# A fused attention, MoE and FFN kernel: stores moved to another queue, small loads moved later, a table's product moved one step

## The chip, the cores and the metric

The kernel runs on one core of a Trainium2 chip. A core has five engines that run their own instruction streams: PE (TensorE, matmuls and transposes), ACT (ScalarE), DVE (VectorE), POOL (GpSimd) and SP (SyncE, which here only starts transfers). The metric is device time in microseconds (us) of one execution.

## The reference, cut to what matters

```python
# attention: q, k, v are [4, 8, 576, 64]; heads 0-3 local, 4-7 strided
mask_local = (rel >= 0) & (rel < 32)
mask_strided = (rel >= 0) & (pos[None, :] % 32 == pos[:, None] % 32)
scores = where(mask, q @ k.T / 8, -1e9);  attn = softmax(scores) @ v
x = attn.transpose(0, 2, 1, 3).reshape(2304, 512)
# MoE: 8 experts, top 1, F = 1024
logits = x @ w_gate + modality_bias[modality_id]
e_idx = argmax(logits);  gate_w = softmax(logits)[e_idx]
out[mask_e] = gate_w[mask_e] * (relu(x[mask_e] @ w1[e]) @ w2[e])
# dense FFN, 512 -> 2048 -> 512
h = out @ w_in;  g = where(h > 0, h, exp(min(h, 0)) - 1);  result = g @ w_out
```

## The kernel before

The program has three stages: attention (to about 131 us of the trace), the mixture of experts (to about 383 us) and the dense FFN (to the end). Every instruction's order on its engine is the order in which the code is written; an engine runs its stream in order and waits where a semaphore says so.

**Attention** runs over 32 steps n, two for each of 16 pairs of heads (four batches; in each, two strided pairs and then two local ones). Step n emits, in this order: S(n), the scores, into two PSUM banks of the tag "S", which has two, so that S(n) has to wait until DVE has copied step n-1's scores out of them (`sm`, L1027) with the mask added; T, the transposes of the next pair's `qn` and `kn` (L996, bank `ps_tr`, one half before and one after PT), which ACT copies to `qt` and `kt`; PT(n-2), the transposes of the exponentials; L, the router's logits; X(n-5), transposes of finished rows of x, which ACT casts to `xh` and DVE to `xl`; PV(n-3), the product with v, which DVE scales into `xs`; and the exponential of step n-1 on ACT. POOL subtracts the row maxima (L1035). The loads of a pair (`load_pair`, L890 and L895) are started on SP some five steps ahead. When a batch's rows of a pair of heads are ready in `xs`, `emit_PV` stores them to `x_dram` in HBM, on SP (L1103 strided, L1106 local; 12 stores).

**The router's early work** stands in a background generator. `bg()` emits its next piece, `bg.step()` starts a new step, and a yielded STEP ends what may be emitted in this step. It starts in step 21: `choose` (logits to expert), `early` (which expert and where each token goes, then a table of the first job's rows, made by `onehot` and `oa` on DVE, `A` on POOL and nine small matmuls `tab_ps` on PE, L404, whose result DVE turns into `idx` and `gates`), then four indirect gathers on POOL (`xg`, L459), the casts of the first weights (`split_to`), four scalings by the gate on DVE (L463) and four groups of transposes on PE (`trans`, L474, bank `x_ps` of the tag "T", which has two). The table's product is the call `finish()`. In the kernel before, steps 25 to 31 hold: 25 `finish` and gathers 0 and 1; 26 gathers 2 and 3 and `split_to(0)`; 27 `split_to(1)`; 28 scalings 0 and 1; 29 scalings 2 and 3 and `trans` 0; 30 `trans` 1 and 2; 31 `trans` 3.

**The router's small inputs** are `wgf` (the gate's weights, 16 KB), `mi` (modality ids, 18 KB) and `bb` (the two bias rows). They are loaded on ACT's queue as its first instructions; `wgs` (first used by L in step 10) and `mf` come from them at once, and `emit_bias` in step 5 makes the bias of each token, with three operations and the constants of the router on POOL.

**The MoE** runs as a stream of numbered pieces, and the list `plan` puts other work (the last attention steps, the other tables, gathers, transposes) before the piece of a given number.

Transfers started from SP and ACT signal their landing on eight semaphores in turn, DMAHW0 to DMAHW7. An instruction that starts a transfer waits until the last one on its semaphore has landed.

Of the kernel before, what the change touches and what calls it, by code (L numbers as in the profile page):

```python
# [73 lines left out]
class Background:  # L74
# [99 lines left out]
class Router:  # L174
# [105 lines left out]
    def early(self, pool, chosen, more):  # L280

        V = self.tc.nc.vector
        t = lambda shape, dt, name: pool.tile(shape, dt, name=name)
        rank = self.rank(NE, 1)
        yield
        key = t([128, E], F32, "key")
        kmax = t([128, 1], F32, "kmax")
        z = t([128, NE, E], F32, "z")
        pr = t([128, NE, E], F32, "pr")
        no = t([128, NE], F32, "no")  # L290
        sh = [128, NE, E]
# [12 lines left out]
        yield Background.STEP
        V.reduce_sum(pos, pr, axis=AX.X)
        V.tensor_tensor(key[0:1], key[0:1], self.rev[0:1], ALU.mult)
        yield
        V.tensor_scalar(pos, pos, 4096.0, None, ALU.add)
        V.reduce_max(kmax[0:1], key[0:1], axis=AX.X)
        yield  # L310
        V.tensor_scalar(self.star, kmax[0:1], -1.0, float(E), ALU.mult, ALU.add)
        chosen()
        yield from self.split_places(0, NE)
        yield Background.STEP
        onehot = self.new_onehot(pool)
        for i, _ in enumerate(self.onehot(0, NE, onehot)):
            yield
        finish = self.table(pool, onehot, 0, NE, 0, 4, 5, self.idx, self.gates, self.tc.nc.gpsimd)
        more()
        yield Background.STEP  # L320
        finish()
        yield

        def others():

            V.tensor_scalar(no, pos, 512.0, None, ALU.is_ge)
            V.tensor_scalar(self.oh[:, 0:NE, 0], pos, 512.0, None, ALU.is_lt)
            V.tensor_tensor(oh, oh, no.unsqueeze(2).to_broadcast(sh), ALU.mult)

        self.others = others  # L330
# [84 lines left out]
def ffn(tc, ctx, x_dram, part_dram, ident, router, conv, bank, w1, w2, out, run_attention):  # L415
# [187 lines left out]
    def early():  # L603
        STEP = Background.STEP
        yield from router.choose(0, NE)
        yield STEP
        yield from router.early(r_p, lambda: fetch_to(0), lambda: fetch_to(1))
        for c in range(4):
            gather(jobs[0], c)
            yield STEP if c == 1 else None  # L610
        split_to(0)
        fetch_to(2)
        yield STEP
        split_to(1)
        fetch_to(3)
        yield STEP
        for c in range(4):
            scale(jobs[0], c)
            yield STEP if c == 1 else None
        for kk in range(4):  # L620
            trans(jobs[0], kk)
            yield STEP if kk % 2 == 0 else None

    bg.early = early
    at = run_attention(bg)
# [17 lines left out]
    def more_tables(c0):  # L643
        fin.append(router.table(late[0], oh[0], 0, NT, c0, c0 + 16, 5, idx, gate))
# [21 lines left out]
    def stream():  # L666
# [31 lines left out]


    plan = [  # L700
        (2, lambda: at.PV(29)), (1, lambda: at.X(27)), (2, lambda: at.X(28)), (2, lambda: at.PT(30)),
        (3, lambda: at.PV(30)), (3, lambda: at.X(29)), (3, lambda: at.PT(31)),
        (4, lambda: at.PV(31)), (4, lambda: at.X(30)),
# [1 line left out]
        (10, lambda: at.lg(NE, NT)), (5, lambda: router.others()), (10, lambda: run(router.choose(NE, NT))), (10, close_b),  # L705
        (14, lambda: run(router.place(r_p))), (16, first_tables),
        (28, table), (28, lambda: router.blocks(r_p)), (28, lambda: new_job(1)), (66, open_y),
        (84, lambda: more_tables(20)), (100, table), (104, lambda: more_tables(36)), (116, table), (164, table),
    ]
    plan += [(120 + 4 * i, lambda i=i: dense(i)) for i in range(NT // 3 + 1)]  # L710
    plan += [(28, lambda c=c: gather(jobs[1], c)) for c in range(4)]
    plan += [(38, lambda c=c: scale(jobs[1], c)) for c in range(4)]
    plan += [(n, lambda kk=kk: trans(jobs[1], kk)) for kk, n in enumerate((47, 50, 53, 55))]
# [144 lines left out]
def attention(tc, bg, q, k, v, mod, mbias, wg, x_dram, ident, router, bank):  # L858
# [105 lines left out]
    m0 = const.tile([128, NT], F32, name="m0")  # L964
    bias = const.tile([128, NT, E], F32, name="bias")
    bt = const.tile([128, NT, E], F32, name="bt")
    nc.scalar.dma_start(wgf, wg.rearrange("(k p) e -> p k e", p=128))
    nc.scalar.dma_start(mi, mod.bitcast(I32).rearrange("(i p two) -> i p two", p=128, two=2))
    nc.scalar.dma_start(bb, mbias.rearrange("m e -> (m e)").partition_broadcast(128).rearrange("p (m e) -> p m e", m=2))

    nc.scalar.copy(wgs[:, :, 0:E], wgf)
    nc.vector.tensor_tensor(wgs[:, :, E:2 * E], wgf, wgs[:, :, 0:E].bitcast(F32), ALU.subtract)
    nc.vector.tensor_copy(mf, mi[:, :, 0])

    def emit_bias():
        pm = bank("T", "pm", 128, NT)
# [7 lines left out]
        router.constants()  # L984

    st = {}

    def emit_T(pi, j):

# [58 lines left out]
            nc.scalar.copy(pt[0:w, nj * r:nj * r + nj], ps)  # L1048
        st[n] = pt

    xs = {}

    xh, xl = (xt_p.tile([128, 4, S], F32R, name=nm) for nm in ("xh", "xl"))
    lgt = const.tile([2 * E, 2 * S], F32, name="lgt")
# [1 line left out]
    def emit_PV(n):  # L1056
        b, pr, s = steps[n]
        m, w, nj = shape(pr)
        pt = st.pop(n)
        key = (b, pr // 2)  # L1060
        if key not in xs:
            xs[key] = xs_p.tile([m, S // m, 4 * D], F32, tag=f"xs{pr // 2}", name="xs")
        c0 = 2 * (pr % 2) * D
        xv = xs[key][:, nj * s:nj * s + nj, c0:c0 + 2 * D]
        rs = m_p.tile([m, 2, nj], F32, tag="rs", name="rs")
        if pr >= 2:
            pss = [bank("P", "ps_v", m, nj, D + 1) for r in range(2)]
        else:

            both = bank("P", "ps_v", m, 2 * nj, D + 1)  # L1070
            pss = [both[:, nj * r:nj * r + nj] for r in range(2)]
        for r in range(2):
            for j in range(nj):
                if pr >= 2:
                    vv = vs[:, 2 * (pr % 2) + j % 2, 4 * s + 2 * (j // 2) + r]
                else:
                    vv = vl[:, nj * s + j, 2 * (pr % 2) + r]
                nc.tensor.matmul(pss[r][:, j], lhsT=pt[:, nj * r + j], rhs=vv, start=True, stop=True)
            if pr >= 2:
                nc.vector.tensor_scalar(rs[:, r], pss[r][:, :, D], 1e-9, None, ALU.add)  # L1080
                bg()
        if pr < 2:
            nc.vector.tensor_scalar(rs.rearrange("p r j -> p (r j)"), both[:, :, D], 1e-9, None, ALU.add)
            bg()
        bg()
        nc.vector.reciprocal(rs, rs)
        bg()
        if pr >= 2:
            for r in range(2):
                o = xv.rearrange("p (g r) (h d) -> p g r h d", r=2, h=2)[:, :, r]  # L1090
                nc.vector.tensor_tensor(o, pss[r][:, :, 0:D].rearrange("p (g h) d -> p g h d", g=2),
                                        rs[:, r].rearrange("p (g h) -> p g h", g=2).unsqueeze(3).to_broadcast([m, 2, 2, D]), ALU.mult)
                bg()
        else:
            nc.vector.tensor_tensor(xv.rearrange("p j (r d) -> p r j d", r=2), both[:, :, 0:D].rearrange("p (r j) d -> p r j d", r=2),
                                    rs.unsqueeze(3).to_broadcast([m, 2, nj, D]), ALU.mult)
            bg()
            bg()
        if pr % 2:
            xb = x_dram[b * S:(b + 1) * S]  # L1100
            if pr >= 2:
                if s == 1:
                    nc.sync.dma_start(xb[:, 4 * D:].rearrange("(m a) c -> m a c", a=G), xs[key])  # L1103
            else:
                g = slice(nj * s, nj * s + nj)
                nc.sync.dma_start(xb[:, 0:4 * D].rearrange("(i p) c -> p i c", p=m)[:, g], xs[key][:, g])  # L1106

    def emit_X(n):

        b, pr, s = steps[n]  # L1110
        m, w, nj = shape(pr)
        c0 = 2 * (pr % 2) * D
        ps = bank("P", "ps_x", 128, nj, m)
        for g in range(nj):
            nc.tensor.transpose(ps[:, g], xs[b, pr // 2][:, nj * s + g, c0:c0 + 2 * D], ident[0:m, 0:m])

        def view(t):
            t = t[:, pr]
            if pr >= 2:
                return t.rearrange("p (m a) -> p a m", a=G)[:, 4 * s:4 * s + 4]  # L1120
            return t.rearrange("p (i m) -> p i m", m=m)[:, nj * s:nj * s + nj]

        nc.scalar.copy(view(xh), ps)
        nc.vector.tensor_tensor(view(xl), ps, view(xh).bitcast(F32), ALU.subtract)
        bg()
        bg()
# [16 lines left out]

    for j in range(4):
        emit_T(0, j)
    NU = len(steps)
    LP, LV, LX = 2, 3, 5
    for n in range(NU):
        emit_S(n)
        if n + 2 < NU:  # L1150
# [16 lines left out]
        bg.step()  # L1167
        if n:
            emit_exp(n - 1)
        if n == 5:  # L1170
            emit_bias()
        if n % 2 == 1:
            p = n // 2 + 3
# [37 lines left out]
```

## Time and profile before

| | |
|---|---|
| median of 3 runs | 790.72 us (789.87 to 791.3) |
| profiled execution | 787.33 us |
| its span, first to last instruction | 785.6 us |
| mean granted clock of PE | 0.989 |
| busy in the span: PE, DVE, ACT, POOL | 762.7, 509.3, 395.9, 103.3 us |

The profile is one execution, taken apart by engine. A view's "idle before" is how long an engine stood still ahead of an instruction, and the name behind the arrow is what ended that. The granted clock is a share of PE's full 2.4 GHz. The profiled execution is 3.4 us shorter than the median of the runs.

### The profile page before, as it was taken

What the parts mean: (1) busy time and instruction counts of PE and PEld (TensorE: products, weight loads), DVE (VectorE), ACT (ScalarE), POOL (GpSimd) and SP (SyncE); (2) the same over time, 40 slices, a digit from 0 to 9 for tenths busy, and PEclk for the clock granted to TensorE, in tenths of its full rate; (3) what the DMA queues carried; (4) which work ended last, traced back from release to release, by engine and by line L of the source; (5) the groups of instructions that cost most, each with busy time, mean ns of one, the idle gap of its engine ahead of it and who ended that gap; (6) DMA issues with size and microseconds to landing.
All of it is one profiled execution on the core that took longest, in us unless ns stands there. A gap on an engine that the chain in (4) does not pass through costs nothing.

```text
span 785.6 us, 12468 instructions
## 1 busy us (share of the span) xinstructions
PE 762.7 (97%) x4513; PEld 636.8 (81%) x4513; DVE 509.3 (65%) x1122; ACT 395.9 (50%) x759; POOL 103.3 (13%) x131
## 2 busy tenths in 40 slices
PE   7999998999999999999999999999999999999995
PEld 6989887888878888888787888888888888888885
DVE  4779888776779777677477575665566454545443
ACT  4667665424435454445466455554465444444342
POOL 4633352121020020000000100001010020101011
PEclk9999979999999999999999999999999999999999
DMA  9588694455566675564332221123133030201111
GB/s 169 134 177 184 144 239 93 138 160 198 167 215 214 190 245 182 187 191 133 110 107 81 95 81 54 40 68 121 40 111 105 0 108 1 94 14 50 58 42 66
DMA packets 100300, 94.35 MB, mean 120 GB/s; under 512 B 45433, under 2 KB 78731, under 8 KB 100235
## 3 DMA queue, kind: packets, MB, share of 16 engines
q1 hardware_dynamic: 95056, 78.79, 35.1%
q0 software_dynamic: 4480, 14.68, 5.3%
q8 instruction: 37, 0.61, 0.3%
q14 instruction: 28, 0.23, 0.1%
q10 hardware_dynamic: 699, 0.04, 0.1%
HBM read 70.95 MB, written 22.54 MB: 119 GB/s over the span
## 4 chain that ended last, share of the span: by engine, by line
PE 44%; DVE 4%; ACT 3%; issue 0%; POOLq 0%; POOL 0%; DVEq 0%; ACTq 0%
PE o_ps L817 8%; PE o_ps L819 7%; PE o_ps L818 7%; PE h_ps L730 7%; PE h_ps L729 7%; PE h_ps L731 7%; DVE r L794 1%; DVE t L793 1%; DVE wl L480 1%; ACT gh L795 1%; ACT wh L479 1%; ACT t L790 0%; ACT e L791 0%; DVE cv_r L158 0%; ACT cv_a L146 0%
## 5 line engine op out<-in xcount | busy, mean ns | idle before, releaser
L793 DVE SCALAR_TENSOR_TENSOR t<-e,t 128x512 f32<-128x512 f32 (+1 forms) x80 | 51.1, 638 | 112.6 <-ACT e L791 112.5
L729 PE MATMUL h_ps<-xh,wh 128*128 128x512 f32 (+1 forms) x320 | 119.1, 372 | 2.0 <-PEq L743 2.0
L731 PE MATMUL h_ps<-xh,wl 128*128 128x512 f32 (+1 forms) x320 | 119.1, 372 | 0.0
L730 PE MATMUL h_ps<-xl,wh 128*128 128x512 f32 (+1 forms) x320 | 119.0, 372 | 0.0
L817 PE MATMUL o_ps<-wh,gh 128*128 128x512 f32 x288 | 113.5, 394 | 0.1
L818 PE MATMUL o_ps<-wl,gh 128*128 128x512 f32 x288 | 113.0, 393 | 0.0
L819 PE MATMUL o_ps<-wh,gl 128*128 128x512 f32 x288 | 112.9, 392 | 0.0
L790 ACT ACTIVATE t<-h_ps 128x512 f32<-128x512 f32 (+1 forms) x80 | 44.2, 552 | 102.2 <-PE h_ps L731 94.7
L795 ACT CAST gh<-r 128x512 fp32r<-128x512 f32 (+1 forms) x80 | 46.2, 578 | 81.7 <-DVE r L794 81.7
L796 DVE TENSOR_TENSOR gl<-r,gh 128x512 fp32r<-128x512 f32 (+1 forms) x80 | 51.1, 639 | 51.5 <-ACT gh L795 51.5
L480 DVE TENSOR_TENSOR wl<-wraw,wh 128x1024 fp32r<-128x1024 f32 x56 | 68.5, 1223 | 11.1 <-ACT wh L479 10.8
L729 PEld LDWEIGHTS h_ps<-xh,wh 128*128 128x128 f32 x320 | 60.4, 189 | 14.0 <-issue 2.4
L730 PEld LDWEIGHTS h_ps<-xl,wh 128*128 128x128 f32 x320 | 60.6, 189 | 11.9
L731 PEld LDWEIGHTS h_ps<-xh,wl 128*128 128x128 f32 x320 | 60.4, 189 | 11.0
L817 PEld LDWEIGHTS o_ps<-wh,gh 128*128 128x128 f32 x288 | 54.2, 188 | 12.7 <-DVE o L828 0.7
L819 PEld LDWEIGHTS o_ps<-wh,gl 128*128 128x128 f32 x288 | 54.2, 188 | 12.2
L515 PE MATMUL y_ps<-hh,wh 128*128 128x512 f32 x160 | 64.0, 400 | 0.0
L496 PE MATMUL h_ps<-xh,wh 128*128 128x512 f32 x160 | 63.6, 398 | 0.0
L818 PEld LDWEIGHTS o_ps<-wl,gh 128*128 128x128 f32 x288 | 54.2, 188 | 11.2
L498 PE MATMUL h_ps<-xh,wl 128*128 128x512 f32 x160 | 62.9, 393 | 0.0
L517 PE MATMUL y_ps<-hh,wl 128*128 128x512 f32 x160 | 62.8, 392 | 0.0
L497 PE MATMUL h_ps<-xl,wh 128*128 128x512 f32 x160 | 62.8, 392 | 0.0
(180 smaller groups left out, 1383.3 us busy)
## 6 DMA issues: line engine op xcount, KB each, us to landing
wraw<-in_moe_w_dram SPq DMA_DIRECT2D x80, 256.0 KB
raw<-in_moe_w_in_dram SPq DMA_DIRECT2D x16, 512.0 KB
raw<-in_moe_w_out_dram SPq DMA_DIRECT2D x16, 512.0 KB
w_f<-cv_r SPq DMA_DIRECT2D x32, 256.0 KB
wraw<-w_f SPq DMA_DIRECT2D x16, 512.0 KB
part_dram<-o POOLq DMA_DIRECT2D x18, 256.0 KB, 3.0
part<-part_dram SPq DMA_DIRECT2D x18, 256.0 KB
qn<-in_q_dram SPq DMA_DIRECT2D x8, 288.0 KB
```

The source lines that it names most:

```text
L480: nc.vector.tensor_tensor(WL[i], raw, WH[i].bitcast(F32), ALU.subtract)
L496: nc.tensor.matmul(ps, lhsT=a, rhs=job.xh[kk], start=kk == 0, stop=False)
L497: nc.tensor.matmul(ps, lhsT=a, rhs=job.xl[kk], start=False, stop=False)
L498: nc.tensor.matmul(ps, lhsT=b, rhs=job.xh[kk], start=False, stop=kk == 3)
L515: nc.tensor.matmul(ps, lhsT=a, rhs=hh, start=f == 0, stop=False)
L517: nc.tensor.matmul(ps, lhsT=b, rhs=hh, start=False, stop=f == NCH - 1)
L729: nc.tensor.matmul(ps[:, 0:n], lhsT=a, rhs=yh, start=kk == 0, stop=False)
L730: nc.tensor.matmul(ps[:, 0:n], lhsT=a, rhs=yl, start=False, stop=False)
L731: nc.tensor.matmul(ps[:, 0:n], lhsT=b, rhs=yh, start=False, stop=kk == 3)
L817: nc.tensor.matmul(ps, lhsT=a, rhs=WH[i][:, 512:1024], start=first, stop=False)
L818: nc.tensor.matmul(ps, lhsT=a, rhs=WL[i][:, 512:1024], start=False, stop=False)
L819: nc.tensor.matmul(ps, lhsT=b, rhs=WH[i][:, 512:1024], start=False, stop=last)
```

## The change

Four things move. (1) The 12 stores of x are collected, and each is started behind the `xh` cast of `emit_X` in the same step: on ACT, apart from the last two, which stay on SP. (2) The three small loads of the router are started in step 2 (behind the exponential of step 1), `wgs` and `mf` are made in step 9 and the bias in step 14. (3) One more STEP stands ahead of `finish()`, so the early table's product is emitted in step 26, and the work behind it is spread anew: all four gathers in step 26, `split_to(0)` in 27, `split_to(1)` and scalings 0 and 1 in 28, scalings 2 and 3 in 29, `trans` 0 in 30, `trans` 1 in 31, and `trans` 2 and 3 in the plan at piece 1. (4) Numbers of the plan for tables and the dense row indices change.

```diff
@@ Router.early
         more()
         yield Background.STEP
+        yield Background.STEP
         finish()
@@ early
         for c in range(4):
             gather(jobs[0], c)
-            yield STEP if c == 1 else None
+            yield STEP if c == 3 else None
         split_to(0)
         fetch_to(2)
         yield STEP
         split_to(1)
         fetch_to(3)
-        yield STEP
+        yield
         for c in range(4):
             scale(jobs[0], c)
-            yield STEP if c == 1 else None
-        for kk in range(4):
+            yield STEP if c % 2 else None
+        for kk in range(2):
             trans(jobs[0], kk)
-            yield STEP if kk % 2 == 0 else None
+            yield STEP
@@ plan
+        (1, lambda: trans(jobs[0], 2)), (1, lambda: trans(jobs[0], 3)),
-        (84, lambda: more_tables(20)), (100, table), (104, lambda: more_tables(36)), (116, table), (164, table),
+        (88, lambda: more_tables(20)), (124, table), (126, lambda: more_tables(36)), (140, table), (190, table),
-    plan += [(120 + 4 * i, lambda i=i: dense(i)) for i in range(NT // 3 + 1)]
+    plan += [(142 + 4 * i, lambda i=i: dense(i)) for i in range(NT // 3 + 1)]
@@ attention: the three dma_start of wgf, mi and bb go into load_router(),
-    nc.scalar.dma_start(wgf, wg.rearrange("(k p) e -> p k e", p=128))
+    def load_router():
+        nc.scalar.dma_start(wgf, wg.rearrange("(k p) e -> p k e", p=128))
...
+    def emit_wgs():
+        nc.scalar.copy(wgs[:, :, 0:E], wgf)
...
@@ emit_PV (both stores)
-                    nc.sync.dma_start(xb[:, 4 * D:].rearrange("(m a) c -> m a c", a=G), xs[key])
+                    stores.append(lambda eng: eng.dma_start(xb[:, 4 * D:].rearrange("(m a) c -> m a c", a=G), xs[key]))
@@ emit_X
         nc.scalar.copy(view(xh), ps)
+        while stores:
+            stores.pop()(nc.scalar if n + LX < NU else nc.sync)
@@ the loop over steps
-        if n == 5:
+        if n == 2:
+            load_router()
+        if n == 9:
+            emit_wgs()
+        if n == 14:
             emit_bias()
```

On ACT, around step 2 of the changed program, `sm` is the exponential of step 1 and the three loads are the router's. The names in brackets are what each instruction waits for.

```order
L1005 COPY qt_149<-ps_tr 128x288 [waits PE_49,Activation_49]
L1045 ACTIVATE sm<-sm 72x576 [waits Pool_49]
L970 DMA wgf<-in_moe_w_gate_dram 128x4x8 [waits DMAHW7_49]
L971 DMA mi<-in_moe_modality_id_dram 18x256 [waits DMAHW0_49]
L972 DMA bb<-in_moe_modality_bias_dram 128x16 [waits DMAHW2_49]
L1007 COPY kt_151<-ps_tr 128x288 [waits PE_49,Activation_49]
L1054 COPY pt_154<-ps_p 72x288 [waits PE_49] x2
```

Before, the three loads were ACT's first instructions and waited for nothing. Now they stand on the semaphores DMAHW7, 0 and 2.

On SP, the loads of v (`vl`, first to fourth of eight) and of pair 3 (`qn`, `kn`) of the program before:

```order
L905 DMA vl<-in_v_dram 96x6x64 [waits DMAHW7_49]
L906 DMA vl<-in_v_dram 32x5x64 [waits DMAHW0_49]
L905 DMA vl<-in_v_dram 96x6x64 [waits DMAHW1_49]
L906 DMA vl<-in_v_dram 32x5x64 [waits DMAHW2_49]
...
L895 DMA qn<-in_q_dram 96x6x64 [waits DMAHW7_49,PE_49]
L895 DMA qn<-in_q_dram 96x6x64 [waits DMAHW0_49]
L895 DMA kn<-in_k_dram 96x6x64 [waits DMAHW1_49,PE_49]
L895 DMA kn<-in_k_dram 96x6x64 [waits DMAHW2_49]
```

The same rows of the changed program:

```order
L907 DMA vl<-in_v_dram 96x6x64 [waits DMAHW4_49]
...
L908 DMA vl<-in_v_dram 32x5x64 [waits DMAHW1_49]
...
L908 DMA vl<-in_v_dram 32x5x64 [waits DMAHW6_49]
L897 DMA qn<-in_q_dram 96x6x64 [waits DMAHW7_49,PE_49]
L897 DMA qn<-in_q_dram 96x6x64 [waits DMAHW0_49]
L897 DMA kn<-in_k_dram 96x6x64 [waits DMAHW1_49,PE_49]
L897 DMA kn<-in_k_dram 96x6x64 [waits DMAHW2_49]
```

The names that pair 3's loads wait on are the same, but before the transfers ahead of them on DMAHW7, 0, 1 and 2 were four `vl` loads; now those on 7, 0 and 2 are the router's three small loads, which ACT starts.

On PE, the end of step 25 before: PV of that step (`ps_v`), the table's product (nine pairs of rows, two of them here) and the scores of step 26.

```order
L1115 MATMUL ps_x<-ident,xs 128x96 x3
L1078 MATMUL ps_v<-vl,pt_154 96x65 x6
L404 LDWEIGHTS onehot
L404 MATMUL tab_ps<-A,onehot 128x20
...
L404 LDWEIGHTS onehot
L404 MATMUL tab_ps<-A,onehot 128x20
L1021 MATMUL ps_sc_1987<-kt_152,qt_150 72x72
L1021 MATMUL ps_sc_1988<-kt_152,qt_150 72x72
```

And after, the end of steps 25 and 26:

```order
L1084 MATMUL ps_v<-vl,pt_154 96x65 x6
L1027 MATMUL ps_sc_1967<-kt_152,qt_150 72x72
L1027 MATMUL ps_sc_1968<-kt_152,qt_150 72x72
...
L1121 MATMUL ps_x<-ident,xs 128x96 x3
L1084 MATMUL ps_v<-vl,pt_155 96x65 x6
L405 LDWEIGHTS onehot
L405 MATMUL tab_ps<-A,onehot 128x20
...
L405 MATMUL tab_ps<-A,onehot 128x20
L1027 MATMUL ps_sc_2047<-kt_152,qt_150 72x72
```

The product (`tab_ps`) has moved from the end of step 25 to the end of step 26; the scores of step 26 now stand directly behind PV of step 25.

On DVE, the order around it is the same in both, here after the change: `xs` of PV, the one-hot rows, `oa`, and then the masked copies `sm` that empty the score banks.

```order
L1101 TENSOR_TENSOR xs<-ps_v,rs 96x2x3x64 [waits DVE_49]
L385 TENSOR_SCALAR onehot<-iota,pos_lof 128x128 x9
L398 TENSOR_TENSOR oa<-iota,pos_hi 128x9x4
L1033 TENSOR_TENSOR sm<-ps_sc_1905,mask_s 72x288 [waits PE_49]
L1033 TENSOR_TENSOR sm<-ps_sc_1906,mask_s 72x288 [waits PE_49]
```

Nothing has moved there.

## Rows read from the trace of the kernel before

**Rows 1.** The page's first part: busy us, share, instructions.

```profile
PE 762.7 (97%) x4513; PEld 636.8 (81%) x4513; DVE 509.3 (65%) x1122; ACT 395.9 (50%) x759; POOL 103.3 (13%) x131
```

**Rows 2.** PE's waits over the span: total, times, longest us.

```profile
PE x_ps L474 <- DVE xg L463: 1.8, 1, 1.8
...
PE x_ps L474 <- DVE tab_sb L406: 1.0, 1, 1.0
...
PE ps_p L1047 <- ACT sm L1039: 0.5, 1, 0.5
```

**Rows 3.** PE's timeline, steps 2, 4 and 12: start, us, what, [idle <-releaser].

```profile
14.47 0.71 PE L996 MATMUL ps_tr<-ident,qn 96*128 96x96 f32 x3 [0.29 <-DMA qn<-in_q_dram]
...
22.43 0.47 PE L996 MATMUL ps_tr<-ident,qn 96*128 96x96 f32 x3
...
49.72 0.44 PE L996 MATMUL ps_tr<-ident,qn 96*128 96x96 f32 x3 [0.95 <-DMA qn<-in_q_dram]
```

**Rows 4.** ACT's timeline, start and step 2.

```profile
0.81 0.43 ACTq L967 DMA_DIRECT2D wgf<-in_moe_w_gate_dram  x1
1.27 0.71 ACTq L968 DMA_DIRECT2D mi<-in_moe_modality_id_dram  x1
...
17.01 0.68 ACT L1039 ACTIVATE sm<-sm 72x576 f32<-72x576 f32 x1
18.56 0.40 ACT L1001 COPY kt<-ps_tr 128x288 f32<-128x288 f32 x1 [0.86 <-PE ps_tr L996]
```

**Rows 5.** DVE's timeline at the start.

```profile
6.13 0.35 DVE L973 CAST mf<-mi 18x128 f32<-18x128 int32 x1 [1.04 <-DMA mi<-in_moe_modality_id_dram]
```

**Rows 6.** SP's timeline of DMA issues, to 45 us.

```profile
9.16 1.54 SPq L895 DMA_DIRECT2D qn<-in_q_dram  x2
...
16.79 1.95 SPq L895 DMA_DIRECT2D qn<-in_q_dram  x2
...
21.48 0.35 SPq L890 DMA_DIRECT2D kn<-in_k_dram  x1
33.22 0.85 SPq L1103 DMA_DIRECT2D x_dram<-xs  x1
...
44.11 1.29 SPq L895 DMA_DIRECT2D qn<-in_q_dram  x2
```

**Rows 7.** DMA issues of one kind: KB, median us to landing.

```profile
part_dram<-o POOLq DMA_DIRECT2D x18, 256.0 KB, 3.0
```

**Rows 8.** PE's timeline, end of step 25.

```profile
99.67 1.19 PE L1078 MATMUL ps_v<-vl,pt 128*96 128x65 f32 x12
102.24 0.37 PE L404 MATMUL tab_ps<-A,onehot 128*128 128x20 bf16 x9 [1.38 <-POOL A L399]
102.54 0.74 PE L1021 MATMUL ps_sc<-kt,qt 64*72 64x72 f32 x16
```

**Rows 9.** DVE's timeline, step 25.

```profile
99.91 1.54 DVE L384 TENSOR_SCALAR onehot<-iota,pos_lof 128x128 bf16<-128x128 bf16 x9
...
101.47 0.81 DVE L1027 TENSOR_TENSOR sm<-ps_sc,mask_s 72x288 f32<-72x288 f32 x2
```

**Rows 10.** Windows: us, busy PE, PEld, DVE, ACT, POOL, clock, DMA share, GB/s.

```profile
16.00:19.00 3.00, 3.00 (x31) 2.65 (x30) 1.07 (x3) 1.88 (x6) 1.04 (x1) 1.00 1.18 194
93.80:97.50 3.70, 3.43 (x48) 3.14 (x46) 3.56 (x21) 2.37 (x7) 1.47 (x1) 1.00 0.80 201
102.50:107.60 5.10, 5.10 (x50) 4.91 (x46) 4.14 (x13) 2.83 (x7) 3.49 (x4) 0.58 0.73 211
107.60:113.30 5.70, 5.70 (x50) 5.42 (x49) 4.13 (x9) 4.16 (x8) 5.13 (x4) 0.50 1.10 258
124.00:128.00 4.00, 3.79 (x45) 3.33 (x46) 2.93 (x16) 2.40 (x5) 0.36 (x1) 1.00 0.13 49
```

**Rows 11.** POOL's timeline, first and last of four gathers.

```profile
104.96 1.19 POOL L459 DMA_INDIRECT xg<-x_dram,idx  x1 [0.51 <-DVE gates L410]
...
111.08 0.96 POOL L459 DMA_INDIRECT xg<-x_dram,idx  x1 [0.30 <-issue]
```

More of the change, by code (lines that the diff above doesn't have):

```diff
@@ L966, in attention @@
     bt = const.tile([128, NT, E], F32, name="bt")
-    nc.scalar.dma_start(wgf, wg.rearrange("(k p) e -> p k e", p=128))
[L968 to L973, printed above, removed]
+    def load_router():
+        nc.scalar.dma_start(wgf, wg.rearrange("(k p) e -> p k e", p=128))
+        nc.scalar.dma_start(mi, mod.bitcast(I32).rearrange("(i p two) -> i p two", p=128, two=2))
+        nc.scalar.dma_start(bb, mbias.rearrange("m e -> (m e)").partition_broadcast(128).rearrange("p (m e) -> p m e", m=2))
+    def emit_wgs():
+        nc.scalar.copy(wgs[:, :, 0:E], wgf)
+        nc.vector.tensor_tensor(wgs[:, :, E:2 * E], wgf, wgs[:, :, 0:E].bitcast(F32), ALU.subtract)
+        nc.vector.tensor_copy(mf, mi[:, :, 0])
     def emit_bias():
@@ L986, in attention @@
     st = {}
+    NU = len(steps)
+    LP, LV, LX = 2, 3, 5
     def emit_T(pi, j):
@@ L1049, in emit_PT @@
         st[n] = pt
-    xs = {}
+    xs, stores = {}, []
     xh, xl = (xt_p.tile([128, 4, S], F32R, name=nm) for nm in ("xh", "xl"))
@@ L1102, in emit_PV @@
                 if s == 1:
-                    nc.sync.dma_start(xb[:, 4 * D:].rearrange("(m a) c -> m a c", a=G), xs[key])
+                    stores.append(lambda eng: eng.dma_start(xb[:, 4 * D:].rearrange("(m a) c -> m a c", a=G), xs[key]))
             else:
                 g = slice(nj * s, nj * s + nj)
-                nc.sync.dma_start(xb[:, 0:4 * D].rearrange("(i p) c -> p i c", p=m)[:, g], xs[key][:, g])
+                stores.append(lambda eng: eng.dma_start(xb[:, 0:4 * D].rearrange("(i p) c -> p i c", p=m)[:, g], xs[key][:, g]))
     def emit_X(n):
@@ L1145, in attention @@
         emit_T(0, j)
-    NU = len(steps)
-    LP, LV, LX = 2, 3, 5
     for n in range(NU):
```

## The prediction

> **What bounds the kernel now.** I read the page's first part and then the waits of the matmul engine PE. PE is busy for 762.7 of 785.6 us [rows 1], so only two things can move the time: the few places where PE idles, and the speed at which it runs. PE's waits come next, each with what ended it; those of 0.3 to 1.8 us that this change might touch are in [rows 2, 3, 8], and a learner should see that nearly all lie in the first 150 us. I then read, for each of them, the engine that releases PE: the start on ACT, DVE and SP [rows 4 to 6], and steps 25 to 30, where the router's early work runs beside attention [rows 8, 9, 11]. Last I read the granted clock [rows 10]: it is 1.00 in step 24 and 0.58 and 0.50 in steps 26 and 27, directly after PE's idle time before 102.24 [rows 8]. 0.50 is the lower of its two levels, 1.2 GHz. Steps 26 and 27 take 5.1 and 5.7 us against 3.7 for step 24: 5.1 + 5.7 - 2 x 3.7 = 3.4 us lost to the clock. After 150 us the change alters nothing but the places of the tables.
>
> **The change, part by part.**
>
> *Small loads leave the start: -0.3 us (0 to -0.3).* PE waits 0.29 us at 14.47 for the second half of `qn` of the first local pair [rows 3]. Three small loads shared the DMA engines with the loads ahead of it. Without them I let that wait go. They move to step 2, behind exp(1) on ACT.
>
> *They come back in SP's way at step 2: +3.0 us (1.7 to 5.1).* The order rows show that each transfer waits for the one before it on its semaphore, of eight. Before, pair 3's `qn` and `kn` waited only for `vl` loads, and its `qn` was issued at 16.79 [rows 6]; PE took it at 22.43 without a wait [rows 3]. After, the halves of `qn` stand behind wgf and mi, and the second half of `kn` behind bb. exp(1) ends at 17.01 + 0.68 = 17.69 [rows 4], say 17.4 with the 0.3 gained; mi's issue follows wgf's by 1.27 - 0.81 = 0.46 [rows 4], so it begins at 17.85. At the start mi was used 6.13 - 1.27 = 4.86 us after its issue [rows 4, 5]. The short bound is the 3.0 us median of the `part_dram` stores [rows 7]. So mi lands between 20.85 and 22.71, and only then does SP issue the second half of `qn`. The first local pair's second half was issued at 9.16 + 1.54/2 = 9.93 [rows 6] and used at 14.47, 4.54 us later; short bound again 3.0. `qn` is there between 23.85 and 27.25. PE wants it at 22.43 - 0.3 = 22.13: a wait of 1.7 to 5.1 us. I take 3.0: mi's load is like its own at the start, since the DMA engines are full at 16 to 19 us (a share of 1.18) [rows 10], which gives 22.71; but nothing else is queued behind it on SP, so the second half is nearer the short 3.0, which makes 3.6; with both short it is 1.7. Behind the waiting `qn` on SP stand `kn` and the next two pairs; PE takes those in later steps, which the wait delays as much. The three issues on ACT (0.43 + 0.71 us, and a third that I put between them) make 1.7 us and lie partly in the gap in which ACT waits for PE, 0.86 us at 18.56 [rows 4]; the rest delays a copy whose reader has a step's time. Their cost I set at 0; without that cover it would be 0.8.
>
> *Stores of x on ACT: -0.95 us (0 to -0.95).* On SP the store of L1103 holds everything behind it until 33.22, 11.4 us after the load ahead of it (21.48 + 0.35) [rows 6], and so pair 7's `qn` is issued only at 44.11 and PE waits 0.95 us at 49.72 [rows 3]. Ten of twelve stores leave that queue and each costs ACT its issue, 0.85 us at 33.22 [rows 6]. They stand behind the `xh` copy, whose input PE transposed from the same `xs` a step or more later than the store's data was ready, so they wait for nothing; ACT idles about as long on PE's transposes, as at 18.56 [rows 4]. Uncovered, ten stores of 0.85 us would put 8.5 us on ACT, most of which its gaps take, since it idles in each step. The Trainium skill (DMA: Bandwidth & Descriptors, "Issuing engines are not separate DMA queues") says that starting transfers on several engines saves only the sequencer's time to start them. By that rule alone this part would be worth about 0, the other bound. The trace differs: the loss is not the start of a transfer but the wait of a blocked queue.
>
> *`emit_bias` from step 5 to 14: 0 (-0.5 to +0.5).* Its three GpSimd operations and the constants delay the softmax's subtraction, and PE waits 0.5 us once for that [rows 2]; later they delay another step alike.
>
> *Early product one step later: -0.3 us (0 to -1.4).* PE waits 1.38 us at 102.24 for A [rows 8]. But A is not the only late thing: DVE runs `onehot` and `oa` from 99.91 to 101.47 and only then the masked copies of step 25, 101.47 to 102.28 [rows 9]. S(26) needs both banks that these two copies free. The changed order keeps DVE's sequence, so PE idles from 100.86 (99.67 + 1.19 [rows 8]) to the first copy's end at about 101.9, does one matmul, and idles again to 102.28. The product's 0.3 us of PE go behind step 26. The gain is 102.54 - 102.28 = 0.3; the other end is the whole wait.
>
> *Transposes one step after their scaling: -1.8; gathers and late transposes: +0.5 (0 to 1).* The 1.8 us wait of `x_ps` on the scaled `xg` [rows 2] goes, since trans 0 now follows all scaling by a step. Against it, four gathers run in one go on POOL instead of two and two. The four took from 104.96 to 111.08 + 0.96 = 112.04, 7.1 us, with one subtraction of the softmax between them [rows 11]. Step 27's softmax subtraction now stands behind them, and PE needs it two steps later: up to 1 us late, or nothing. Transposes 2 and 3 now run against two banks that ACT and DVE must empty at the join with the next stage.
>
> *Tables elsewhere in the plan: -1.0 us (0 to -1.0).* The 1.0 us wait of `x_ps` on `tab_sb` [rows 2] comes from a product directly ahead of two transposes on the same two banks; the new times part them.
>
> Sum without the clock: -0.3 + 3.0 - 0.95 + 0 - 0.3 - 1.8 + 0.5 - 1.0 = **-0.85 us**.
>
> *The clock: -1.4 us (-3.4 to +3.4).* At 102.24 PE idled 1.38 us and the clock fell; in the 1.8 us of [rows 2], which ended at 124.14, it did not: 1.00 from 124 to 128 [rows 10]. So such a gap only sometimes lets it fall. After the change the gap is split, 1.0 and 0.4: I take the fall as gone, -3.4. But a wait of 3 us stands at 22.1, just after PE reached speed: the same three transposes take 0.71 us at 14.47 and 0.47 at 22.43 [rows 3]. (This is read from durations; the clock's row prints 1.00 at 16 to 19 us already [rows 10].) That wait is longer than either gap, and I add 2.0, between 0 and another 3.4. Together -1.4.
>
> Total -0.85 - 1.4 = -2.25. The profiled execution took 787.33 us, 3.4 below the median of 790.72; I apply the difference to the median: 790.72 - 2.25 = **788.5 us**. A measurement here tells changes of 0.2% (1.6 us) from none.
>
> **Rivals.** *R1, slower.* The load of pair 3 comes late enough that PE falls to half speed for two steps (+3.4), and the fall at 103 comes again. Then the sum is -0.85 + (w - 3.0) + 3.4, w being the wait: with w = 3.6, +3.15, or 793.9 us. It is slower by more than 1.6 us from w = 2.1 on. For it: the semaphores in the order rows, and the gap's length. Against it: a gap of 1.8 that cost no clock. *R2, the early product's wait stays whole with its fall of the clock, and the start loses none*: -0.85, 789.9 us; for it, DVE's rows. *R3, the small loads land fast* (w = 1.7), no clock lost at the start, none at 103: -0.85 - 1.3 - 3.4 = -5.55, 785.2 us.
>
> **How the numbers follow.** The forecast has 0.40, R1 0.22, R2 0.20, R3 0.18. The forecast's own range is 786 to 790.5. Leaving out the ends of R1 and of R3, the range is 784.0 to 794.0. Faster by over 0.2%: 0.32 of the forecast and all of R3, 0.50. Within: most of R2 and the rest of the forecast, 0.27. Slower: R1 nearly whole and a little of R2, 0.23.
>
> **What would show it.** Right: a wait of PE on `qn` of 1.7 to 5 us near 22 us, with SP's `qn` issued at 20 us or later; no wait at 49 us; no wait of `tab_ps` on A, but one of `ps_sc` on DVE near 101; no waits of `x_ps` on `xg` and `tab_sb`; a granted clock near 1.00 in steps 26 and 27. Wrong: no `qn` wait near 22 us; a new wait for the softmax of step 27; half speed again after 103.

## The result, and the profile after

The changed kernel took 782.81 us (782.33 to 784.26, 4 executions) against 790.43 us for the kernel before (4 executions): a ratio of 0.9917 with a 95% interval of 0.9896 to 0.9937. That is 7.6 us faster by the medians, 5.0 to 8.2 us by the interval. The forecast was 788.5 us in a range of 784.0 to 794.0: the sign was right, the size was a third of the measured one, and the time lies below the range.

The two profiled executions stand closer: 784.26 us against 787.33, so only 3.1 of the 7.6 us lie between the two traces. The profiled execution of the kernel before is 3.1 us below its median, and that of the changed kernel 1.5 above its own. The prediction took such a difference as a fixed offset.

PE's waits of the changed kernel (total, times, longest, in us), to be held against [rows 2]:

```profile
PE ps_p L1053 <- ACT sm L1045: 2.1, 2, 1.4
...
PE x_ps L475 <- DVE xl L469: 1.2, 1, 1.2
PE ps_sc L1027 <- DVE sm L1033: 0.8, 1, 0.8
...
PE ps_l L1141 <- ACT kt L1007: 0.3, 1, 0.3
```

The waits of `x_ps` on `xg` and on `tab_sb` are gone, and that of `tab_ps` on A too. In their place stand two waits of the softmax (0.6 us in step 17, behind the moved bias; 1.4 us in step 29, behind the four gathers), 0.8 us of the scores on DVE, and 1.2 us of the last transposes on `xl`.

PE's timeline, at the places that answer to [rows 3] and [rows 8]:

```profile
22.51 0.71 PE L1002 MATMUL ps_tr<-ident,qn 96*128 96x96 f32 x3
...
50.13 0.47 PE L1002 MATMUL ps_tr<-ident,qn 96*128 96x96 f32 x3
...
103.62 1.01 PE L1027 MATMUL ps_sc<-kt,qt 64*72 64x72 f32 x16 [0.78 <-DVE sm L1033]
...
106.88 0.38 PE L405 MATMUL tab_ps<-A,onehot 128*128 128x20 bf16 x9
...
117.59 0.69 PE L1053 MATMUL ps_p<-ident,sm 72*72 72x72 f32 x8 [1.44 <-ACT sm L1045]
```

At 22.51 there is no wait on `qn`, though one of 3 us was forecast. At 50.13 the wait of 0.95 us is gone, as forecast. Step 26 (103.62) now waits on DVE's masked copies, as forecast: 0.78 us, with 0.25 us a little earlier, ahead of PV of step 25.

The windows that answer to [rows 10] (steps 24, 26 and 27; the clock is the third column from the end):

```profile
95.40:99.10 3.70, 3.42 (x48) 3.14 (x47) 3.56 (x21) 2.75 (x7) 1.47 (x1) 1.00 0.58 159
103.60:107.20 3.60, 3.58 (x56) 3.40 (x56) 3.33 (x9) 2.14 (x6) 1.28 (x2) 1.00 1.25 241
107.20:110.50 3.30, 3.30 (x54) 3.00 (x51) 3.06 (x12) 2.17 (x7) 2.31 (x2) 1.00 1.06 239
```

The clock stays at 1.00 and the steps take 3.6 and 3.3 us, where they took 5.1 and 5.7. At the start it went the other way: the three transposes at 22.51 take 0.71 us, against 0.47 at 22.43 before, so PE reached full speed later in this execution (read from these durations; the clock's column prints 1.00 there already). S(5) starts at 26.50 us here and at 24.62 before.

### The profile page after: what moved, and what is told of

The parts are those of the page before. It is cut to its first block, busy times and chain, and to the rows that moved or that the text cites. A ratio compares the mean times of both kernels' runs of the same rounds, so it can differ in the third digit from the quotient of the medians.

```text
span 782.5 us, 12469 instructions
## 1 busy us (share of the span) xinstructions
PE 762.0 (97%) x4513; PEld 634.9 (81%) x4513; DVE 509.4 (65%) x1122; ACT 395.9 (51%) x759; POOL 103.2 (13%) x131
## 4 chain that ended last, share of the span: by engine, by line
PE 44%; DVE 4%; ACT 3%; issue 0%; POOLq 0%; POOL 0%; DVEq 0%; ACTq 0%
PE o_ps L819 8%; PE o_ps L820 7%; PE o_ps L821 7%; PE h_ps L732 7%; PE h_ps L731 7%; PE h_ps L733 7%; DVE r L796 1%; DVE t L795 1%; DVE wl L481 1%; ACT gh L797 1%; ACT wh L480 1%; ACT t L792 0%; ACT e L793 0%; DVE cv_r L158 0%; ACT cv_a L146 0%
```

## The experiments

Times below are medians; a ratio is to executions of the kernel before that were timed beside it, and 0.001 of it is 0.79 us.

**One part alone, on the kernel before.** The four parts are those of the change.

```diff
@@ p1_stores: the collected stores alone
         nc.scalar.copy(view(xh), ps)
+        while stores:
+            stores.pop()(nc.scalar if n + LX < NU else nc.sync)
@@ p2_loads: the small loads, their use and the bias alone
-        if n == 5:
+        if n == 2:
+            load_router()
+        if n == 9:
+            emit_wgs()
+        if n == 14:
             emit_bias()
@@ p3_early: this, the STEPs of early() and trans 2 and 3 in the plan alone
         more()
         yield Background.STEP
+        yield Background.STEP
         finish()
@@ p4_plan: the numbers of the plan for tables and dense() alone
-        (84, lambda: more_tables(20)), (100, table), (104, lambda: more_tables(36)), (116, table), (164, table),
+        (88, lambda: more_tables(20)), (124, table), (126, lambda: more_tables(36)), (140, table), (190, table),
```

*p1_stores.* 

> The kernel before with the stores of x on ACT's queue alone. Theory A (the gain of the whole change is mostly the clock, which no longer falls near 103 us): the 0.95 us wait on qn at 49.7 us goes and nothing else moves, 0 to -1 us; the fall near 103 us stays. Theory B (the waits themselves and the loads brought forward make the gain): -2 us or more here.

*p2_loads.* 

> The kernel before with only the router's small loads in step 2, used from step 9, bias in step 14. Theory A: the start comes 0.6 us earlier, no wait on pair 3's qn, but PE stays longer at half speed in steps 4 and 5, so 0 to +3 us. Rival, the prediction's step: PE waits 1.7 to 5 us on qn near 22 us. Second rival: the longer slow start was chance of one execution, then -0.6 us.

*p3_early.* 

> The kernel before with only the early table's product one step later and the work behind it spread anew. Theory A: the granted clock stays near 1.00 in steps 26 and 27, about -4 us there and -0.5 from the waits around 124 us: -4 to -5 us. Theory B: the clock falls again and only the waits are saved, 0 to -1 us.

*p4_plan.* 

> The kernel before with only the new plan numbers for tables and the dense indices. Theory A: the 1.0 us wait of x_ps on tab_sb near 229 us goes, -1 us. Theory B (the timed executions of the kernel before lose 3 us to the clock in a place that its profiled one did not, and it is this one): -3 to -4 us.

| part alone | median us | ratio (95%) | us by the ratio | the prediction's terms |
|---|---|---|---|---|
| p1_stores | 787.37 | 0.9973 (0.9955 to 0.9990) | -2.1 | -0.95 |
| p2_loads | 789.88 | 1.0002 (0.9989 to 1.0016) | +0.2 | -0.3 + 3.0 + 2.0 (clock) = +4.7 |
| p3_early | 785.48 | 0.9951 (0.9933 to 0.9968) | -3.9 | -0.3 - 1.8 + 0.5 - 3.4 (clock) = -5.0 |
| p4_plan | 787.93 | 0.9977 (0.9957 to 0.9998) | -1.8 | -1.0 |
| sum | | | -7.6 | -2.25 |

By the ratios the parts sum to -7.6 us where the whole has -6.6; by the medians they sum to -9.5 where the whole has -7.6. So they add up roughly; whether they act on one another these sums can't tell. The term that is far off is that of the loads. Of the two theories p3's -3.9 us fits A (-4 to -5, nearly all of it the clock near 103 us) and p1's -2.1 fits B (-2 or more), so neither holds alone. Yet p3's profile still has half speed near 103 us. Windows of p3_early, where the product is later and the gap before S(26) is 1.11 us:

```profile
104.00:106.00 2.00, 2.00 (x18) 2.00 (x17) 1.83 (x7) 1.72 (x5) 1.03 (x1) 0.53 0.93 277
...
108.00:110.00 2.00, 2.00 (x23) 1.87 (x24) 1.86 (x8) 0.21 (x1) 0.74 (x1) 0.50 1.09 283
...
112.00:114.00 2.00, 2.00 (x18) 1.88 (x18) 0.62 (x2) 1.62 (x3) 1.66 (x2) 0.50 0.89 200
...
124.00:126.00 2.00, 2.00 (x28) 1.87 (x26) 2.00 (x13) 1.88 (x4) 0.32 (x1) 1.00 0.26 82
126.00:128.00 2.00, 2.00 (x21) 1.45 (x19) 1.93 (x12) 0.72 (x3) 1.34 (x1) 1.00 0.00 0
```

It is fast all the same, and from 122 us on it has no half speed but at the program's end, as all the profiles have. The profiles of p1, p2 and p4, which keep the old early work, have it in both places. This is p4_plan, PE's timeline and the windows behind its wait:

```profile
122.92 0.85 PE L474 MATMUL x_ps<-ident,xg 128*128 128x128 f32 x2 [1.81 <-DVE xg L463]
```

```profile
122.00:124.00 2.00, 1.01 (x4) 0.59 (x6) 1.26 (x4) 0.19 (x1) 0.00 (x0) 0.85 0.56 192
124.00:126.00 2.00, 2.00 (x17) 1.72 (x16) 1.26 (x6) 0.39 (x1) 0.00 (x0) 0.50 0.00 0
...
128.00:130.00 2.00, 2.00 (x14) 2.00 (x14) 1.50 (x6) 0.56 (x2) 0.42 (x1) 0.50 0.00 0
130.00:132.00 2.00, 2.00 (x25) 1.63 (x24) 1.65 (x6) 1.13 (x3) 0.00 (x0) 0.95 0.18 48
```

So half speed does follow the 1.8 us gap of [rows 2]. The profiled execution of the kernel before, in which it did not, was an exception. From here on the theory was C: a gap of PE lets the clock fall in a share of the executions, and the share grows with the gap.

**One part undone, and the first attempt to better it.** a_same is the changed kernel itself.

```diff
@@ u1_stores: the changed kernel with the stores in emit_PV, on SP, as before
-        while stores:
-            stores.pop()(nc.scalar if n + LX < NU else nc.sync)
@@ u3_early: the changed kernel with early(), its STEPs and trans 2 and 3 as before
         yield Background.STEP
-        yield Background.STEP
         finish()
@@ v1_spread: the changed kernel with router.constants() out of emit_bias
-        router.constants()
...
-            yield STEP if c == 3 else None
+            yield STEP if c == 1 else None
-        (1, lambda: trans(jobs[0], 2)), (1, lambda: trans(jobs[0], 3)),
+        (1, lambda: trans(jobs[0], 2)), (2, lambda: trans(jobs[0], 3)),
-        if n == 14:
+        if n == 13:
             emit_bias()
+        if n == 16:
+            router.constants()
```

*a_same.* 

> The changed kernel, unaltered, for more executions and a second profile. Theory C (an idle gap of PE of 1.4 to 1.8 us lets the clock fall in most executions, a gap under 1.1 us in few): no half speed from 100 to 135 us, about 783 us, 7 us below before. Rival (the rise at the start and the falls are chance in each execution): a stretch of half speed near 104 us, and single times spread over 5 us and more.

*u1_stores.* 

> The changed kernel with the stores of x back on SP's queue, the rest kept. If the stores' part adds up as when made alone: 2.1 us above the changed kernel, with a wait of PE on qn near 50 us of about 1 us. If what it gave alone was mostly chance of the clock: 1 us above.

*u3_early.* 

> The changed kernel with the early table's product, the gathers and the transposes back in their old steps. Theory C: both gaps return (about 1.4 us at 103, 1.8 us at 126) and with them two stretches of half speed, 6 to 7 us above the changed kernel. Rival (the part alone gave 4 us): 4 us above, one stretch.

*v1_spread.* 

> The changed kernel with gathers 2 and 3 a step later, the last transposes of job 0 a piece apart, and the router's constants three steps after its bias. It takes away the waits that the changed kernel has anew: PE on the softmax of step 27 (1.4 us), on the exponential near 70 us (0.6), on xl near 131 us (1.2). If these are on the path: 2 to 3 us below the changed kernel. If DVE, which is full there, then holds PE back instead: 0 to 1 us.

Measured: a_same 782.55 us (0.9910), u1_stores 785.08 (0.9923), u3_early 788.25 (0.9966), v1_spread 781.67 (0.9885, interval 0.9851 to 0.9920). Undoing the stores costs 2.5 us by the medians and 1.0 by the ratios, with waits on `qn` of 0.38 and 1.42 us in its trace. Undoing the early part costs 5.7 us by the medians and 4.4 by the ratios, between theory C's 6 to 7 and the rival's 4; its profile has one stretch of half speed, near 124 us. v1_spread takes the softmax waits away and is 0.9 us faster than a_same by the medians; the intervals overlap. a_same also gave a second profile of the changed kernel, and in it the clock does fall behind the 0.78 us gap, and PE does wait on pair 3's `qn`:

```profile
100.00:102.00 2.00, 1.22 (x20) 0.94 (x19) 1.90 (x7) 0.01 (x1) 0.49 (x1) 1.00 1.07 282
102.00:104.00 2.00, 2.00 (x17) 2.00 (x17) 1.93 (x7) 1.24 (x4) 1.15 (x1) 0.56 1.35 207
104.00:106.00 2.00, 2.00 (x15) 2.00 (x14) 1.22 (x3) 1.43 (x3) 0.91 (x1) 0.50 1.00 201
...
112.00:114.00 2.00, 2.00 (x26) 1.76 (x25) 1.04 (x5) 0.55 (x2) 1.98 (x2) 0.88 0.88 278
```

```profile
20.60 0.90 PE L1027 MATMUL ps_sc<-kt,qt 64*96 64x128 f32 x12
22.37 0.44 PE L1002 MATMUL ps_tr<-ident,qn 96*128 96x96 f32 x3 [0.88 <-DMA qn<-in_q_dram]
```

The profile shown at the top was thus better at 103 us and worse at the start; a_same is the opposite, and the two took 784.26 and 784.45 us.

**The gap near 124 us by itself.** b_same is the kernel before, unaltered.

```diff
@@ m1_trans_later: the kernel before, trans 0 and 1 in step 30, 2 and 3 in step 31
             scale(jobs[0], c)
-            yield STEP if c == 1 else None
+            yield STEP if c % 2 else None
         for kk in range(4):
             trans(jobs[0], kk)
-            yield STEP if kk % 2 == 0 else None
+            yield STEP if kk % 2 else None
@@ g1_trans_soon: the changed kernel, trans 0 back in step 29
             scale(jobs[0], c)
-            yield STEP if c % 2 else None
+            yield STEP if c == 1 else None
@@ v2_split: v1_spread, six one-hot operations a step ahead of the last three
-            yield
+            yield Background.STEP if i == 1 else None
         more()
-        yield Background.STEP
         yield Background.STEP
         finish()
```

*b_same.* 

> The kernel before, unaltered, for a second profile. Theory C: its 1.8 us gap of PE near 124 us lets the clock fall in most executions, the profiled one shown in the prediction being an exception: half speed for some 10 us behind that gap, and step 30 and 31 some 2 to 3 us longer than there. Rival: no fall there, and the 3 us between the profiled and the timed executions lie elsewhere.

*m1_trans_later.* 

> The kernel before with the four groups of transposes of job 0 one step later (two in step 30, two in step 31) and nothing else. It takes the 1.8 us gap near 124 us away and leaves the table's product and the gap near 102 us. Theory C: no half speed from 120 to 135 us, 3 to 5 us faster, about what the whole early part gave alone (3.9). Rival (the early product's own step matters most): about 1 us faster.

*g1_trans_soon.* 

> The changed kernel with the first group of transposes back in the step of its scaling (29), the rest kept. Theory C: PE waits 1 to 2 us for the scaled rows again and the clock falls behind it in most executions: 2 to 5 us above the changed kernel's 782.6. Rival: 0 to 1 us above.

*v2_split.* 

> The kernel of the spread gathers and constants, with the nine one-hot operations split over two steps (six and three), the product in the same step as in the changed kernel. It takes 1 us of DVE out of the way of the masked copies of step 25. Theory C: the 0.8 us gap near 101 us shrinks to under 0.4, no half speed there, 1 to 3 us below the kernel it starts from (781.7). Rival (that gap is only moved to the next step, DVE being full): 0.

Measured: b_same 789.96 us (0.9995), m1_trans_later 785.94 (0.9960, 0.9944 to 0.9975), g1_trans_soon 786.68 (0.9954), v2_split 779.72 (0.9864, 0.9839 to 0.9890). The second profile of the kernel before, at the same gap and behind it:

```profile
123.29 0.73 PE L474 MATMUL x_ps<-ident,xg 128*128 128x128 f32 x2 [1.81 <-DVE xg L463]
```

```profile
122.00:124.00 2.00, 0.65 (x4) 0.34 (x4) 1.60 (x5) 0.00 (x0) 0.00 (x0) 1.00 0.51 149
124.00:126.00 2.00, 2.00 (x26) 1.85 (x26) 1.32 (x8) 1.25 (x4) 0.00 (x0) 0.88 0.01 4
126.00:128.00 2.00, 2.00 (x18) 2.00 (x18) 1.55 (x10) 1.27 (x3) 1.21 (x1) 0.50 0.00 0
128.00:130.00 2.00, 2.00 (x19) 1.71 (x18) 1.67 (x5) 1.17 (x2) 0.26 (x1) 0.77 0.00 0
130.00:132.00 2.00, 2.00 (x26) 1.98 (x25) 1.97 (x14) 1.42 (x4) 0.00 (x0) 1.00 0.56 136
```

It is the same program with the same gap (1.81 us), and now the clock is at half, 1.2 GHz, for some 3 us behind it; near 103 us, where it fell in [rows 10], it stays up this time. And where it stays up, a wait shows that the slow steps hid. PE's transposes of the last pair's `qn` in step 28, in the kernel before, in b_same and in m1:

```profile
114.23 0.47 PE L996 MATMUL ps_tr<-ident,qn 96*128 96x96 f32 x3
```

```profile
113.43 0.44 PE L996 MATMUL ps_tr<-ident,qn 96*128 96x96 f32 x3 [1.82 <-DMA qn<-in_q_dram]
```

```profile
112.44 0.44 PE L996 MATMUL ps_tr<-ident,qn 96*128 96x96 f32 x3 [1.55 <-DMA qn<-in_q_dram]
```

SP started that load at 106.19, 105.89 and 105.42 us in these three, behind the stores of x; in p1, with the stores on ACT, it did so at 99.09.

m1 moves nothing but the transposes and gains 3.2 us by the ratio (2.0 to 4.4), nearly the whole of p3's 3.9. That leaves 0.7 us for the product one step later, inside the two intervals. Windows of m1 where the gap was:

```profile
122.00:124.00 2.00, 2.00 (x27) 1.89 (x24) 2.00 (x15) 1.81 (x5) 0.00 (x0) 1.00 0.52 183
124.00:126.00 2.00, 2.00 (x27) 1.75 (x26) 1.93 (x7) 1.35 (x4) 1.47 (x1) 1.00 0.00 0
126.00:128.00 2.00, 2.00 (x22) 1.95 (x21) 2.00 (x13) 1.89 (x5) 0.00 (x0) 1.00 0.30 80
```

g1 puts the gap back into the changed kernel, and half speed follows it again; it is 4.1 us slower than a_same by the medians and 3.5 by the ratios (in this profile its 1.4 us softmax gap in step 29 is followed by half speed too):

```profile
124.03 0.72 PE L475 MATMUL x_ps<-ident,xg 128*128 128x128 f32 x2 [1.42 <-DVE xg L464]
```

```profile
126.00:128.00 2.00, 2.00 (x18) 2.00 (x17) 1.52 (x14) 1.68 (x4) 0.47 (x1) 0.50 0.00 0
```

**The loads once more, and the better kernel again.** a_again and v2_again are the changed kernel and v2_split, unaltered.

```diff
@@ l1_loads_first (from the changed kernel), v3_loads_first (from v2_split)
+    load_router()
+    emit_wgs()
+
     def emit_bias():
@@ the loop over steps
-        if n == 2:
-            load_router()
-        if n == 9:
-            emit_wgs()
```

*l1_loads_first.* 

> The changed kernel with the router's small loads and their use back at the start (the bias stays in step 14). If the loads in step 2 cost a longer stretch of half speed in half of the executions: 1 to 2 us faster than the changed kernel on the same chip, S(5) at 25 us or before. If the late rise is chance: equal or up to 0.6 us slower, from the start alone.

*a_again.* 

> The changed kernel, unaltered, beside the one with the loads at the start: about 782.6 us, and one more profile of the start; S(5) at 24.5 or at 26.5 us.

*v3_loads_first.* 

> The kernel with the split one-hot operations, with the small loads and their use back at the start. If the loads in step 2 cost clock: 1 to 2 us faster than that kernel on the same chip. If not: equal or up to 0.6 us slower.

*v2_again.* 

> The kernel with the split one-hot operations, unaltered, for more executions: about 779.7 us, some 3 us below the changed kernel on the same chip if its shorter gap near 100 us keeps the clock up more often; equal if its five executions were lucky.

Measured: l1_loads_first 782.77 us beside a_again 782.73; v3_loads_first 779.81 beside v2_again 780.24. Where the loads stand makes no difference that can be measured. v2_split holds its lead: v2_again is 2.5 us below a_again beside it, as v2_split was 2.8 below a_same's median. The waits of v2_again show what went:

```profile
PE ps_sc L1025 <- DVE mx L1036: 1.7, 7, 0.5
PE h_ps L497 <- DVE xl L468: 0.6, 1, 0.6
```

```profile
100.06 1.01 PE L1025 MATMUL ps_sc<-kt,qt 64*72 64x72 f32 x16 [0.18 <-DVE sm L1031]
```

From 20 us on no wait in attention is above 0.5 us any more (the second row is at the start of the MoE), and the gap before S(26) is 0.18 us.

**What all eighteen profiles say of the clock.** Each row counts profiles with a gap of PE at that place and those in which a stretch of half speed followed it. A PE wait of the size named stands in the trace of each, and the stretch was read from windows of 2 us.

| place and gap | profiles | half speed behind it |
|---|---|---|
| before S(26) or the product, 0.9 to 1.4 us (before, b_same, p1 to p4, u1, u3, m1) | 9 | 6 |
| before S(26), 0.8 us (after, a_same, a_again, v1, g1, l1) | 6 | 1 |
| before S(26), 0.2 us (v2_split, v2_again, v3) | 3 | 0 |
| before the transposes near 124 us, 1.4 to 1.8 us (before, b_same, p1, p2, p4, u3, g1) | 7 | 6 |
| the same place with the gap gone | 11 | 0 |
| softmax in step 29, 1.4 us (after, a_again, g1, l1) | 4 | 2 |
| `qn` near 50 us, 0.95 to 1.4 us (before, p2, p3, u1), and near 113 us, 1.6 to 1.8 us (b_same, m1) | 6 | 0 |
| the last transposes on `xl` near 130 us, 1.2 us (after, a_same, a_again, l1, p3, u1) | 6 | 0 |
| `x_ps` on `tab_sb` near 229 us, 1.0 us (before, b_same, p1, p2, p3, m1) | 6 | 0 |
| where the dense FFN begins, near 380 us, 1.2 to 2.1 us (all) | 18 | 3 |

The last four rows matter as much as the others: gaps of the same length elsewhere were hardly ever followed by half speed, the 1.82 us near 113 us in b_same not at all. So theory C, with the length of the gap alone, doesn't hold across places; what sets the places near 103, 117 and 124 us apart stays open. One of the three falls near 380 us is in the profile of the kernel before, where the prediction did not look: PE waits 1.96 us at 381.87, and some 3 us at half speed follow.

```profile
381.87 0.47 PE L729 MATMUL h_ps<-xh,wh 128*128 128x512 f32 x1 [1.96 <-PEq L743]
```

```profile
382.00:384.00 2.00, 2.00 (x8) 1.58 (x9) 1.02 (x2) 1.33 (x3) 0.00 (x0) 0.80 0.04 12
384.00:386.00 2.00, 2.00 (x7) 1.52 (x6) 1.06 (x3) 1.60 (x3) 0.00 (x0) 0.50 0.03 8
```

**What all timed executions say of the clock.** A profile is one execution, but each timed execution has its mean granted clock too. In the profiles that mean follows the time at half speed ahead of the end: 0.996 to 0.998 with none, 0.995 with some 3 us, 0.993 with 7, 0.990 with 10, 0.986 or 0.987 with 17. Every stretch near 103 us was 10 us or longer, so an execution at 0.994 or more had none there.

| kernel | executions | median of the mean clock | at 0.994 or more |
|---|---|---|---|
| before, with b_same | 108 | 0.988 | 7 |
| early work as before (p1, p2, p4, u3) | 48 | 0.987 | 5 |
| transposes later, product as before (m1) | 12 | 0.992 | 1 |
| product later, transposes soon (g1) | 12 | 0.993 | 1 |
| both later and nothing else (p3) | 12 | 0.997 | 8 |
| the changed kernel with the stores on SP (u1) | 6 | 0.991 | 1 |
| the changed kernel (with a_same, a_again) | 22 | 0.997 | 20 |
| v1 | 6 | 0.995 | 4 |
| l1, v2_split, v2_again, v3 | 23 | 0.997 | 23 |

So m1's profile, without any half speed ahead of the end, was the only such one of its 12 executions, p3's with it one of 4 in 12 and a_same's one of 2 in 22; by the medians of m1, g1 and p3 each of the two moves, of the transposes and of the product, takes away about half of the lost clock. p3's eight executions at 0.996 or more have a median of 784.0 us, its other four 787.5. The kernel before gains less where its clock stays up (788.4 us in the 7, 789.9 in all 108), which fits the hidden wait of 1.6 to 1.8 us. p1, whose stores are on ACT, is 3.6 us below the kernel before beside it among the executions at 0.991 or more (5 and 9 of them) and 0.5 us among those at 0.987 or less (7 and 12).

## Why the prediction was wrong

The result lies 1.2 us under the range. Step by step:

- **"They come back in SP's way at step 2: +3.0 us": this is the step that failed, and with it the 2.0 us of clock hung on it.** The mechanism is there: SP's `qn` does wait for wgf (1.5 us, the row below). Its size was wrong at each link. I let wgf start when exp(1) ends, at 17.4 us; ACT started it at 15.86, before exp(1) itself began. mi followed at 16.34 and not 17.85. SP issued both halves of `qn` from 19.15 us on, where I had the second at 20.85 to 22.71. PE waited 0.88 us on it in a_same, 0.52 in u1 and nothing in the profile after. The part alone measured +0.2 us (-0.9 to +1.3) where I had +4.7, which is most of the 5.3 us between the forecast and the medians' -7.6.

ACT's and SP's timelines and SP's waits in the changed kernel:

```profile
15.86 0.44 ACTq L970 DMA_DIRECT2D wgf<-in_moe_w_gate_dram  x1
16.10 0.68 ACT L1045 ACTIVATE sm<-sm 72x576 f32<-72x576 f32 x1
16.34 0.94 ACTq L971 DMA_DIRECT2D mi<-in_moe_modality_id_dram  x1
```

```profile
17.02 0.51 SPq L908 DMA_DIRECT2D vl<-in_v_dram  x1
19.15 0.86 SPq L897 DMA_DIRECT2D qn<-in_q_dram  x2
```

```profile
SPq L897 <- DMA wgf<-in_moe_w_gate_dram: 1.5, 1, 1.5
```

- **"In the 1.8 us of [rows 2], which ended at 124.14, it did not": one execution taken for a rule.** Half speed follows that gap in 6 of 7 profiles. I priced it at its own 1.8 us; taking it away alone gave 3.2 us. The fall near 103, which I priced at 3.4 us and took as gone, is gone in 20 of 22 executions of the changed kernel, but only in 8 of 12 of p3, where it costs 3.5 us by p3's own executions. p3 comes out at -3.9 against my -5.0, so near in part by luck: the gap near 124 us gave more than I said, and a third of p3's executions kept the fall that I took as gone. The split gap on which I had hung this, 1.0 and 0.4 us, came out as 0.25 and 0.78 with PV between them, and half speed follows it in 1 of 6 profiles.
- **"I apply the difference to the median."** The 3.4 us between the profiled execution and the median had a cause that I did not look for, and it stays open. The fall near 124 us is missing in that trace and present in all five others with the old transposes, but the trace has the fall near 380 us that most lack, and its mean clock of 0.989 is about the kernel's median of 0.988. So the amount of half speed does not account for the difference.
- **Stores, -0.95: right mechanism, too small.** The wait went as described. Alone it measured -2.1 us (-0.8 to -3.6). In other profiles with the stores on SP, `qn` is late twice between 40 and 51 us, by 0.55 and 1.30 us in p2 and by 0.38 and 1.42 in u1, and where the clock stays up near 103 us it is late by 1.6 to 1.8 us near 113 us as well (b_same, m1). With the stores on ACT the gap near 103 us is also cut in two by PV of step 25: 0.25 and 0.95 us in p1 and u3 against 1.38, and 0.25 and 0.78 in the changed kernel against 1.11 in p3 and u1. That these make up what p1 gained beyond 0.95 is argued and not shown. The loss was the wait of a blocked queue (11.4 us in [rows 6]), and it went with the stores. The Trainium skill (DMA: Bandwidth & Descriptors, "Issuing engines are not separate DMA queues") says that starting transfers on several engines saves only the time that it takes to start them; p1's gain goes beyond that.
- **Tables, -1.0:** the wait went; -1.8 us measured (-0.2 to -3.4), which holds the forecast.
- **Early product, -0.3:** right. The gap moved from `tab_ps` to `ps_sc` and shrank from 1.38 to 1.03 us (0.78 + 0.25) in the profile after and to 1.11 in p3's, because DVE's order was kept. v2_split, which splits that work of DVE, takes it to 0.18 us.
- **Gathers and late transposes, +0.5:** too small by the waits. The new ones are 1.44 us on the softmax and 1.18 on `xl`; no run takes these two away alone (v1, which takes the softmax waits away, is 0.9 us faster).
- **Small loads out of the start, -0.3:** the wait at 14.47 went in the profile after (13.53, no wait), yet moving the loads back to the start cost nothing (l1, v3).

R3 came nearest, 785.2 us: no clock lost, and the loads at 1.7 us, which is still more than they cost.

## What to carry to other kernels

A profile is one draw: where it lies some tenths of a per cent off the median of the timed runs, take a second one before adding differences to either, and hold its mean granted clock against those of the timed executions. On a nearly full PE an idle gap of 1 to 2 us costs its own length and, at some places, a stretch of half speed behind it in most executions: 14 of 20 gaps of 0.9 us and more near 103, 117 and 124 us, but 3 of 36 elsewhere (from 40 us on). So read from the traces which gaps have one, and remove those first. A lost stretch of clock can hide a late load, which shows once the clock stays up. A transfer that an engine starts behind a computation can be started before that computation begins (15.86 against 16.10 us), so its time is not the end of the instruction ahead.

## What the runs showed that I had not expected

- The stretch at half speed near 124 us was some 3 us long in b_same and some 7 in p4 (from the windows shown: 0.88, 0.50, 0.77 of 2 us each, against 0.85, three of 0.50, 0.95), behind the same gap of 1.81 us.
- The time of the rise at the start scatters as well: S(5) began between 24.08 and 27.24 us in the eighteen profiles. It was over 26 us in 4 of 10 with the loads in step 2 and in 0 of 8 with the loads at the start. The timed runs show no difference from it, so whether the loads play a part in it stays open.
- A late rise hides a late load: S(4) takes 1.60 us in the profile after and `qn` comes in time; it takes 0.90 in a_same, and PE waits 0.88 us. That may be one reason why the loads' place cost nothing; it is argued, not shown.
